# Moving the maxima's transfers from SyncE to ScalarE, and a new order of the last stores and evictions

## The chip, the cores and the metric

The kernel runs on one core of one Trainium2 chip. The metric is the device time of one execution, in microseconds. Before the change the median of three runs is 1801.67 us (1796.04 to 1801.83).

Five engines run their own instruction streams and meet through semaphores: TensorE (PE in the profile), VectorE (DVE), ScalarE (ACT), GpSimd (POOL) and SyncE (SP, which here only issues transfers).

## The reference, cut to what matters

The input x has 2048 rows of 640. Two things are computed from it and mixed by a gate of one number per row:

```
g = sigmoid((x * gate_w).sum(-1))
a = Cr @ (x @ Wr.T) - Ci @ (x @ Wi.T)          # real part of a 2-D Fourier transform; Cr, Ci 2048 x 2048
q = x @ wq  (32 heads of 20);  k = x @ wk;  v = x @ wv   (one key and value head for all)
p = softmax(q k^T / sqrt(20));  b = (p v) @ wo
out = g * a + (1 - g) * b
```

All of it is float32. The kernel reaches that with a high and a low part of each operand and three products.

## The kernel before, in words

**Attention.** The 32 heads are worked in 16 pairs, and each pair in two halves of the rows, so that there are 32 stages, numbered v = 2p + qh. For each stage two passes over the scores are made. Pass "a" (`a_unit`, L227, matmul L235) computes scores and VectorE reduces each 128 x 512 block to its row maximum (L242). When a stage's 64 blocks are done, `a_reduce` and `a_final` (L244 to L267) join them, transpose, and split the negated maximum into a high and a low part (tile m3). The maxima are then needed as two more rows of the query tile: m3 is stored to a scratch tensor `m_d` in DRAM (L258), and four small reads bring it back, as rows 60, 61, 124 and 125 of `qs[v]` (L261 to L267). Pass "b" (`b_unit`, L854, matmul L857) computes the scores with those rows, so the maximum is already subtracted, and ScalarE takes the exponential (L865). `av_step` multiplies the result with the values (L869). So no matmul of pass b of stage v can start before the four reads have landed.

**The loop.** A stage is eight rounds (L976). A round follows a written list (`AB15`, `Y16`, `Y12`, `N12`, L924 to L942): eight pass-b blocks and eight pass-a blocks (none in `N12`), some 12 to 16 pairs of half-width matmuls of the other work ("y0", "y1"), two evictions on ScalarE (E0, E1) and two av steps (V). Pass a runs ahead: the maxima of stage v + 1 are done at the end of the sixth round of stage v, so two rounds lie between them and their first use. Four times a round `tick` (L216) moves a counter on and calls what `later(n, f, ...)` (L213) has put off by n ticks; it is called behind the 1st, 3rd, 5th and 7th pass-b block.

**The other work** is the Fourier part, a generator (`f_stream`, L778) from which matmuls are drawn: first the product along the hidden dimension (`ab_stream`), then seven products with the 2048 x 2048 matrices, whose blocks `load_c` fetches (512 KB each) and `split_c` splits on GpSimd, and last the output projection of the first 512 columns (L823 on).

**The order.** Line 49 puts TensorE, ScalarE, VectorE and GpSimd under a manual schedule: their instructions run in the order in which the code issues them. SyncE isn't in that list; a planner of the framework orders its transfers. Every transfer of the kernel before goes through SyncE (`move`, L109).

**The end.** The last pair of heads has its sums late. `finish_half` stores them, `finish_last` takes the reciprocals on VectorE and stores them, `load_rec` reads them back spread over partitions, `split_last` multiplies them in and splits the product, and `o_group` does the last 128 columns of the projection: three matmuls, one eviction into the accumulator (L664), one store of the output (L665). The first 16 groups (rows 0 to 1023) run right behind the loop, the other 16 when the second half's reciprocals are there. `split_last` for the first half is called inside the loop, behind the last but one round (kk = 6 of the last stage, L1011 to L1013).

Of the kernel before, what the change touches and what calls it, by code (L numbers as in the profile page):

```python
# [17 lines left out]
P = 128  # L18
# [15 lines left out]
def kernel(  # L34
# [71 lines left out]
    def words(ap):  # L106
        return ap.bitcast(F32) if ap.dtype == F32R else ap

    def move(dst, src):  # L109
        nc.sync.dma_start(words(dst), words(src))  # L110

    def split(raw, hi, lo):
        nc.scalar.activation(hi, raw, AF.Copy)
# [102 lines left out]
    def tick():  # L216
        clock["n"] += 1
        due = [t for t in todo if t[0] <= clock["n"]]
        todo[:] = [t for t in todo if t[0] > clock["n"]]
        for _, f, args in due:  # L220
            f(*args)
# [27 lines left out]
    def a_final(v):  # L249

        m3 = sml[0].tile([P, 3, 32], F32, name="m3")
        nc.vector.transpose(m3[:, 0], mxr[v % 2])
        mt = m3[:, 0].rearrange("p (t o) -> p t o", o=1)
        both = m3[:, :2].rearrange("p i t -> p t i")
        with nc.allow_low_precision(reason="high and low part of the maximum"):
            nc.vector.tensor_reduce(m3[:, 1].bitcast(F32R), mt, axis=AX.X, op=ALU.max, negate=True)
            nc.vector.tensor_reduce(m3[:, 2].bitcast(F32R), both, axis=AX.X, op=ALU.add, negate=True)
        move(m_d[v], m3[:, 1:])  # L258

        m_v = m_d[v].rearrange("(g r) i t -> r i g t", g=4)  # L260
        for hh in range(2):  # L261
            for i in range(2):
                r = 64 * hh + 60 + i
                move(
                    qs[v][r : r + 1].rearrange("o (b g t) -> o b g t", g=4, t=32),
                    m_v[hh * QB : (hh + 1) * QB, i : i + 1].rearrange("b o g t -> o b g t"),
                )  # L267


    sml = []  # L270
    chores = []
# [373 lines left out]
    def split_last(qh, k, n):  # L645
        cs = slice(k * QT // n, (k + 1) * QT // n)
        if k == 0:
            last_hl[qh] = [c_slot(2 * qh + z, [P, QT], F32R, "osp") for z in range(2)]
        o, r = last_o[qh]
        h, l = last_hl[qh]  # L650
        nc.vector.tensor_tensor(o[:, cs], o[:, cs], r[:, cs], op=ALU.mult)
        nc.vector.tensor_copy(h[:, cs], o[:, cs])
        nc.vector.tensor_tensor(l[:, cs], o[:, cs], h[:, cs].bitcast(F32), op=ALU.subtract)

    orot = Rot(["S0", "S1", "S2", "S3", "S4", "F0", "F1"])

    def o_group(tb, e):
        qh, k = divmod(tb, SJ)
        tk = slice(k * P, (k + 1) * P)
        ps = orot(f"o_{tb}_{e}")[:, :HALF]  # L660
        h, l = last_hl[qh]
        mm3(ps, h[:, tk], l[:, tk], *wos[OC, e], 1, 0)
        t = acc[tb][:, e]
        nc.vector.scalar_tensor_tensor(t, ps, omg[:, tb : tb + 1], t, op0=ALU.mult, op1=ALU.add)  # L664
        move(out[tb * P : (tb + 1) * P, e * HALF : (e + 1) * HALF], t)  # L665


    class Halves:
# [66 lines left out]
    def ab_stream():  # L735

        groups = []
        for e in range(2):
            for m in range(SJ):
                k = NT * e + 2 * m  # L740
                turn = [(z, i) for z in range(2) for i in range(2)]
                if m == (SJ - 1, 0)[e]:
                    turn.sort(key=lambda x: x[1])
                groups += [(e, k + z, i) for z, i in turn]
        ends = {}
        for n, (e, k, i) in enumerate(groups):
            ends["x", k] = n
            ends["w", e, i] = n
        wait = [(ends["x", k - 3], 1, 1, load_x, split_x, (k,)) for k in range(3, len(XSEQ))]
        for i in range(2):  # L750
            wait.append((ends["w", 0, i], 0, 2, load_w, split_w, (i, 1)))
        wait.sort(key=lambda x: x[:2])
        flying = [(0, 1, 1, load_x, split_x, (2,))]
        for n, (e, k, i) in enumerate(groups):
            ps = [bank("F", f"ab_{n}_{g}") if stage["loop"] else lrot(f"ab_{n}_{g}") for g in range(2)]
            ps = [x[:, :HALF] for x in ps]
            xh, xl = x_now[k]
            for c in range(KC):
                wh, wl = w_of(i, c)
                halves.put(ps, xh[:, c], wh, c == 0, False)  # L760
                yield ("put", 1)
                halves.put(ps, xl[:, c], wh, False, False)
                yield ("put", 1)
                halves.put(ps, xh[:, c], wl, False, c == KC - 1)
                if c == KC - 1:
                    ended.append({"ab": (e, XSEQ[k], i), "ps": ps})
                yield ("put", 1)
            for _, _, _, _, f2, args in flying:
                f2(*args[: 1 if f2 is split_w else 2])
            flying = []  # L770
            while wait and wait[0][0] <= n and sum(x[2] for x in flying) + wait[0][2] <= 2:
                flying.append(wait.pop(0))
                flying[-1][3](*flying[-1][5])
            if n == len(groups) - 3:
                load_c(0)
                split_c(0)

    def f_stream():  # L778

        yield from ab_stream()  # L780
        cw.close()
        yp.append(ctx.enter_context(tc.tile_pool(name="yp", bufs=2, side="right")))
        for g in range(NP):
            n, k = divmod(g, NT)
            r, sh = divmod(k, 2)
            name = PRODUCTS[n][0]
            if g == 0:
                load_c(1)
            if g >= 2:
                free_c.append(c_now.pop(g - 2)[2])  # L790
            sum_t(g - 1)
            split_c(g + 1)
            load_c(g + 2)
            split_b(g + NT)
            load_b(g + NT + 1)
            if n == 0 or g == NT:
                load_t(g)
            if n == len(PRODUCTS) - 1:
                if 1 <= k <= KC + 1:
                    split_wo(k - 2) if k > 1 else None  # L800
                    load_wo(k - 1)
                elif k in (12, 14):
                    load_o((k - 12) // 2)
                elif k == 13:
                    split_o(0)
            if sh == 0:
                ps = [bank("F", f"y_{name}_{r}_{z}")[:, :HALF] for z in range(2)]
                parts = [part(z, part_d[x][r]) for z, x in enumerate(READS.get(name, ()))]
            h, l, _ = c_now[g]
            for j in range(SJ):  # L810
                t = ab[n % 2, sh * SJ + j]
                hi, lo = t[:, 0], t[:, 1]
                s0 = sh == 0 and j == 0
                s1 = sh == 1 and j == SJ - 1
                halves.put(ps, h[:, j], hi, s0, False)
                yield ("put", 1)
                halves.put(ps, h[:, j], lo, False, False)
                yield ("put", 1)
                halves.put(ps, l[:, j], hi, False, s1)
                if s1:  # L820
                    ended.append({"y": (name, r, parts), "ps": ps})
                yield ("put", 1)
        for tb in range(NT):  # L823
            for e in range(2):
                if e == 0:
                    split_o(tb + 1)
                else:
                    load_o(tb + 2)
                ps = [bank("F", f"oo_{tb}_{e}_{z}")[:, :HALF] for z in range(2)]
                y0 = part(e, y_d[tb * P : (tb + 1) * P, e * HALF : (e + 1) * HALF])  # L830
                h, l = osp[tb]
                for c in range(OC):
                    wh, wl = wos[c, e]
                    halves.put(ps, h[:, c], wh, c == 0, False)
                    yield ("put", 1)
                    halves.put(ps, h[:, c], wl, False, False)
                    yield ("put", 1)
                    halves.put(ps, l[:, c], wh, False, c == OC - 1)
                    if c == OC - 1:
                        ended.append({"o": (tb, e, y0), "ps": ps})  # L840
                    yield ("put", 1)
# [175 lines left out]

    for i in range(NT):
        tb, e = divmod(i, 2)
        o_group(tb, e)  # L1020
        if i == 1:
            for st in old:
                av_step(*st)
            finish_half(*old[-1][:2])
            load_last(1)
        elif i >= NT - 4:
            tick()
    load_rec(1)
    for i in range(NT):
        tb, e = divmod(i, 2)  # L1030
        if i % 4 == 0:
            split_last(1, i // 4, 4)
        o_group(SJ + tb, e)


# [45 lines left out]
```

## Time and profile before

| | |
|---|---|
| median of the runs | 1801.67 us |
| profiled execution, its time / its span | 1803.36 us / 1801.6 us |
| TensorE matmul busy | 1747.6 us (97%) |
| VectorE busy | 1372.5 us (76%) |
| ScalarE busy | 1243.0 us (69%) |
| GpSimd busy | 1123.1 us (62%) |
| mean granted TensorE clock | 0.985 |
| transfers, all issued by SyncE | 260.52 MB, 145 GB/s |

The busy shares are means over stages that differ. Where an engine's idle time comes from is read from the waits and from the timeline; what a stage loses is read by laying stages with the same number of matmuls side by side. In a row of a timeline the two first numbers are the start and the duration in us, and the bracket at the end says how long the engine was idle before, and what ended it.

### The profile page before, as it was taken

Reading aid. Unit: us, or ns where it says so; the run is one execution under the profiler, and the core shown is the slowest. Engines: PE = TensorE matmul, PEld = TensorE weight load, DVE = VectorE, ACT = ScalarE, POOL = GpSimd, SP = SyncE. Lnnn points to the kernel's source line nnn. Section 1 sums busy time; section 2 is a strip of 40 time slices with the busy share of each in tenths; the row PEclk is TensorE's granted clock in tenths of the full one; section 3 lists DMA queues with packets and bytes.
Section 4 is the critical chain, followed back from the end, with each engine's and each line's share of the span. In section 5 each row is a group of like instructions: output and inputs, shape, how many; then the busy total and the mean of one; then the engine's idle time right before and its main releaser. Section 6 shows DMA issues by size and latency. Waiting matters only on the chain.

```text
span 1801.6 us, 43713 instructions
## 1 busy us (share of the span) xinstructions
PE 1747.6 (97%) x16728; PEld 1246.0 (69%) x16728; DVE 1372.5 (76%) x2301; ACT 1243.0 (69%) x2470; POOL 1123.1 (62%) x983
## 2 busy tenths in 40 slices
PE   8999999999999999999999989999999999999995
PEld 6797767767677677677767667776776666666664
DVE  4498888888788688788868768886888788888814
ACT  3337887887677677577767657666777777788891
POOL 3056563332878656777868897897887443367781
PEclk9999999999999999999999999999999999999998
DMA  7552232222776433456657764654455222132334
GB/s 245 184 168 77 75 98 81 75 77 90 232 232 207 155 108 106 155 191 208 221 175 234 229 218 145 197 182 152 156 175 167 79 82 77 39 89 78 87 102 137
DMA packets 175059, 260.52 MB, mean 145 GB/s; under 512 B 32330, under 2 KB 131146, under 8 KB 174250
## 3 DMA queue, kind: packets, MB, share of 16 engines
q1 hardware_dynamic: 174850, 257.74, 45.7%
q8 instruction: 131, 2.15, 0.5%
q14 instruction: 78, 0.64, 0.1%
HBM read 184.59 MB, written 77.00 MB: 145 GB/s over the span
## 4 chain that ended last, share of the span: by engine, by line
PE 92%; DMA 4%; SPq 1%; POOL 1%; DVE 1%; issue 0%; ACT 0%; DVEq 0%; POOLq 0%; ACTq 0%
PE av L869 25%; PE b L857 18%; PE y_p L680 18%; PE a L235 15%; PE ab L680 7%; PE oo L680 3%; DMA m_d<-m 2%; PE q L118 1%; PE q L120 1%; SPq L110 1%; PE q L119 1%; DMA qs<-m_d 1%; DMA wraw<-in_wq_dram 1%; POOL cl L504 1%; DVE acc L664 0%
## 5 line engine op out<-in xcount | busy, mean ns | idle before, releaser
L242 DVE TENSOR_REDUCE mx<-a 128x1 f32<-128x512 f32 x2048 | 1278.4, 684 | 309.5 <-PE a L235 285.3
L865 ACT ACTIVATE pt<-b 128x512 f32<-128x512 f32 x2048 | 1076.7, 605 | 395.0 <-PE a L235 326.6
L857 PE MATMUL b<-qs,ks 62*128 62x512 f32 x2048 | 782.0, 419 | 23.5 <-DMA qs<-m_d 20.5
L235 PE MATMUL a<-ks,qs 60*128 60x512 f32 x2048 | 728.5, 414 | 0.0
L680 PE MATMUL y_p<-tb,ch 64*128 64x320 f32 x3584 | 642.9, 310 | 0.0
L857 PEld LDWEIGHTS b<-qs,ks 62*128 62x128 f32 x2048 | 355.2, 187 | 251.4 <-DVE mx L242 163.9
L680 PEld LDWEIGHTS y_p<-tb,ch 64*128 64x128 f32 x3584 | 488.6, 188 | 8.6 <-POOL ch L503 0.3
L869 PE MATMUL av<-pt,vsb 128*32 128x512 f32 x4096 | 492.5, 598 | 0.0
L680 PE MATMUL y_p<-tb,cl 64*128 64x320 f32 x1792 | 450.7, 309 | 1.9 <-POOL cl L504 1.9
L235 PEld LDWEIGHTS a<-ks,qs 60*128 60x128 f32 x2048 | 354.2, 186 | 8.3 <-issue 1.1
L722 POOL TENSOR_TENSOR yt<-yt,yu 128x320 f32<-128x320 f32 x88 | 76.6, 870 | 345.1 <-ACT yu L717 325.9
L680 PEld LDWEIGHTS y_p<-tb,cl 64*128 64x128 f32 x1792 | 280.0, 188 | 7.7 <-POOL cl L504 2.1
L504 POOL TENSOR_TENSOR cl<-craw,ch 128x1024 fp32r<-128x1024 f32 x112 | 267.5, 2388 | 9.0
L869 PEld LDWEIGHTS av<-pt,vsb 128*32 128x32 f32 x4096 | 106.8, 109 | 223.7 <-issue 214.9
L722 POOL TENSOR_TENSOR abt<-abt,abu 128x320 f32<-128x320 f32 x64 | 55.8, 871 | 181.0 <-ACT abu L717 170.4
L498 POOL TENSOR_TENSOR craw<-craw 128x1024 f32<-128x1024 f32 x64 | 153.5, 2398 | 0.0
L503 POOL CAST ch<-craw 128x1024 fp32r<-128x1024 f32 x112 | 116.2, 1038 | 12.8 <-PE a L235 6.5
L680 PE MATMUL oo<-wo,osp 64*128 64x320 f32 x768 | 93.2, 307 | 0.0
L680 PEld LDWEIGHTS oo<-wo,osp 64*128 64x128 f32 x768 | 85.8, 186 | 1.8
L522 POOL TENSOR_TENSOR tb<-braw,tb 128x320 fp32r<-128x320 f32 x80 | 70.1, 876 | 6.4
L680 PE MATMUL ab<-wbh,xh 64*128 64x320 f32 x256 | 58.8, 306 | 0.0
L680 PE MATMUL ab<-wbh,xl 64*128 64x320 f32 x256 | 58.5, 305 | 0.0
(111 smaller groups left out, 1622.2 us busy)
## 6 DMA issues: line engine op xcount, KB each, us to landing
craw<-in_cre_dram SPq DMA_DIRECT2D x80, 512.0 KB
craw<-in_cim_dram SPq DMA_DIRECT2D x64, 512.0 KB
s_d<-craw SPq DMA_DIRECT2D x32, 512.0 KB
craw<-s_d SPq DMA_DIRECT2D x32, 512.0 KB
braw<-b_d SPq DMA_DIRECT2D x80, 160.0 KB
xraw<-in_xT_dram SPq DMA_DIRECT2D x32, 320.0 KB
qs<-qh_d SPq DMA_DIRECT2D x128, 80.0 KB
b_d<-abt SPq DMA_DIRECT2D x64, 160.0 KB
```

Source lines behind the costliest of these rows:

```text
L110: nc.sync.dma_start(words(dst), words(src))
L235: nc.tensor.matmul(ps, qs[v][b : b + 60, qb * P : (qb + 1) * P], ks[b : b + 60, c * ROW : (c + 1) * ROW], start=True, stop=True,)
L242: nc.vector.tensor_reduce(mx[v][:, hh, qb, c : c + 1], ps, axis=AX.X, op=ALU.max)
L498: nc.gpsimd.tensor_tensor(raw[0], raw[0], raw[1], op=how)
L503: nc.gpsimd.tensor_copy(h, raw[0])
L504: nc.gpsimd.tensor_tensor(l, raw[0], h.bitcast(F32), op=ALU.subtract)
L522: nc.gpsimd.tensor_tensor(t[:, 1], raw, t[:, 0].bitcast(F32), op=ALU.subtract)
L680: nc.tensor.matmul(ps, w, x, start=start, stop=stop)
L722: nc.gpsimd.tensor_tensor(t0, t0, t1, op=ALU.add)
L857: nc.tensor.matmul(ps, ks[b : b + 62, kc * P : (kc + 1) * P], qs[2 * p + qc // 2][b : b + 62, (qc % 2) * ROW : (qc % 2 + 1) * ROW], start= ...
L865: nc.scalar.activation(t, ps, AF.Exp, scale=SCALE)
L869: nc.tensor.matmul(ps[32 * g : 32 * g + 32, :], vsb[:, kc, :], t, start=first, stop=last)
```

## The change

`a_final` no longer issues its five transfers at once on SyncE. The store to `m_d` is put off by one tick, the reads by 4, 5, 5 and 6 ticks, and ScalarE issues them. `load_c` of the Fourier part is called two ticks later, except that of block 1, which moves into `ab_stream`. In `split_last` the rounding copy goes to ScalarE, and the multiplication goes to GpSimd for all but the first piece. The first 16 output stores are issued by ScalarE, two groups late; the ticks that issue the reciprocals move behind the loop of groups; every third of the last 16 groups is evicted by ScalarE (scaled copy) and GpSimd (addition) instead of VectorE.

```
+    def move_act(dst, src):
+        nc.scalar.dma_start(words(dst), words(src))
...
-        move(m_d[v], m3[:, 1:])
+        later(1, move_act, m_d[v], m3[:, 1:])
...
-                move(
+                later(
+                    4 + hh + i,
+                    move_act,
                     qs[v][r : r + 1].rearrange("o (b g t) -> o b g t", g=4, t=32),
...
-        nc.vector.tensor_tensor(o[:, cs], o[:, cs], r[:, cs], op=ALU.mult)
-        nc.vector.tensor_copy(h[:, cs], o[:, cs])
+        (nc.gpsimd if k else nc.vector).tensor_tensor(o[:, cs], o[:, cs], r[:, cs], op=ALU.mult)
+        nc.scalar.activation(h[:, cs], o[:, cs], AF.Copy)
...
+    def o_store(i, how):
+        tb, e = divmod(i, 2)
+        how(out[tb * P : (tb + 1) * P, e * HALF : (e + 1) * HALF], acc[tb][:, e])
+
-    def o_group(tb, e):
+    def o_group(tb, e, spread):
...
-        nc.vector.scalar_tensor_tensor(t, ps, omg[:, tb : tb + 1], t, op0=ALU.mult, op1=ALU.add)
-        move(out[tb * P : (tb + 1) * P, e * HALF : (e + 1) * HALF], t)
+        if spread:
+            u = yp[0].tile([P, HALF], F32, name="yt")
+            nc.scalar.activation(u, ps, AF.Copy, scale=omg[:, tb : tb + 1])
+            nc.gpsimd.tensor_tensor(t, t, u, op=ALU.add)
+        else:
+            nc.vector.scalar_tensor_tensor(t, ps, omg[:, tb : tb + 1], t, op0=ALU.mult, op1=ALU.add)
...
             if n == len(groups) - 3:
                 load_c(0)
                 split_c(0)
+            elif n == len(groups) - 2:
+                load_c(1)
...
-            if g == 0:
-                load_c(1)
...
-            load_c(g + 2)
+            later(2, load_c, g + 2)
...
     for i in range(NT):
         tb, e = divmod(i, 2)
-        o_group(tb, e)
+        o_group(tb, e, False)
...
-        elif i >= NT - 4:
-            tick()
+        elif i > 1:
+            o_store(i - 2, move_act)
+    for _ in range(4):
+        tick()
     load_rec(1)
+    for i in range(NT - 2, NT):
+        o_store(i, move_act)
     for i in range(NT):
-        tb, e = divmod(i, 2)
         if i % 4 == 0:
             split_last(1, i // 4, 4)
-        o_group(SJ + tb, e)
+        o_group(SJ + i // 2, i % 2, i % 3 == 2)
+        o_store(NT + i, move)
```

## The prediction, made before the result was known

> **What bounds the kernel now.** First the page: the whole span, then the engines, the clock and the chain.
>
> ```profile
> span 1801.6 us, 43713 instructions
> PE 1747.6 (97%) x16728; PEld 1246.0 (69%) x16728; DVE 1372.5 (76%) x2301; ACT 1243.0 (69%) x2470; POOL 1123.1 (62%) x983
> PEclk9999999999999999999999999999999999999998
> PE 92%; DMA 4%; SPq 1%; POOL 1%; DVE 1%; issue 0%; ACT 0%; DVEq 0%; POOLq 0%; ACTq 0%
> ```
>
> TensorE is the bound, and the chain of work runs through it for 92%. So nothing is to be had from a faster helper, only from places where TensorE waits or runs slowly. The groups of instructions (busy time, mean ns of one | idle time before them and what ended most of it) and the matmul timeline say where that is in the loop:
>
> ```profile
> L857 PE MATMUL b<-qs,ks 62*128 62x512 f32 x2048 | 782.0, 419 | 23.5 <-DMA qs<-m_d 20.5
> 599.08 0.76 PE L857 MATMUL b<-qs,ks 62*128 62x512 f32 x1 [3.21 <-DMA qs<-m_d]
> 1073.86 0.76 PE L857 MATMUL b<-qs,ks 62*128 62x512 f32 x1 [4.47 <-DMA qs<-m_d]
> ```
>
> Pass b of some stages waits for the maxima's reads, 20.5 us in all. A stall costs more than its wait: the matmul behind it takes 0.76 us where the mean is 419 ns. So I measure stages whole. These windows run from one start of `a_final`'s transpose to the next; the columns are length, then busy time and count of each engine, then granted clock, DMA share, GB/s.
>
> ```profile
> 430.12:482.57 52.45, 50.57 (x512) 35.60 (x508) 41.28 (x70) 36.74 (x74) 31.11 (x27) 1.00 0.62 195
> 532.74:582.92 50.18, 50.18 (x516) 35.77 (x512) 41.23 (x69) 35.65 (x71) 37.62 (x34) 1.00 0.66 206
> 582.92:639.92 57.00, 53.53 (x516) 38.48 (x512) 41.11 (x69) 36.21 (x71) 33.13 (x31) 0.94 0.47 148
> 740.28:796.45 56.17, 53.40 (x516) 38.62 (x512) 41.36 (x69) 36.28 (x71) 38.13 (x30) 0.94 0.60 194
> 896.86:954.40 57.54, 53.45 (x516) 38.29 (x512) 41.11 (x69) 36.19 (x71) 40.44 (x33) 0.94 0.59 186
> 1004.58:1056.44 51.86, 50.72 (x516) 35.87 (x512) 41.00 (x69) 35.85 (x71) 44.06 (x36) 1.00 0.72 235
> 1056.44:1114.50 58.06, 53.38 (x516) 38.34 (x512) 41.37 (x69) 36.16 (x71) 44.11 (x35) 0.94 0.52 167
> 1214.87:1271.85 56.98, 53.10 (x516) 38.06 (x512) 41.10 (x68) 35.95 (x71) 43.26 (x34) 0.94 0.52 161
> 1421.03:1470.50 49.47, 48.96 (x456) 32.38 (x448) 39.94 (x68) 36.49 (x69) 26.55 (x27) 1.00 0.34 104
> 1470.50:1519.23 48.73, 48.73 (x456) 32.52 (x448) 40.15 (x69) 36.10 (x69) 16.96 (x12) 1.00 0.28 85
> ```
>
> With the same 516 matmuls a stage takes 50.18 us undisturbed and 51.86 to 58.06 us in the six disturbed ones. The long ones have a granted clock of 0.94: half of the loss is the wait, the other half is TensorE being slow behind it.
>
> Why are the maxima late? VectorE, then SyncE's queue, in the stage that ends in the stall at 599:
>
> ```profile
> 583.38 0.22 DVE L257 TENSOR_REDUCE m<-m 128x32 fp32r<-128x64 f32 x1
> 591.48 0.33 SPq L110 DMA_DIRECT2D craw<-in_cim_dram  x1
> 592.38 0.38 SPq L110 DMA_DIRECT2D m_d<-m  x1
> 596.25 2.78 SPq L110 DMA_DIRECT2D qs<-m_d  x4
> ```
>
> The maxima are ready at 583.60 and their store is issued at 592.38, 8.8 us later, behind transfers like the block load at 591.48. The reads follow at 596.25, and TensorE goes on at 599.08, about 1.5 us behind the second read (four take 2.78, so two end near 597.6). Two rounds (12.5 us, a quarter of 50.18) lie between maxima and use, and SyncE's queue eats most of them. The transfers themselves are quick.
>
> **The change part by part, as a sum against the profiled execution** (span 1801.6, time 1803.36, which is 1.69 above the median 1801.67).
>
> *Maxima on ScalarE.* The store comes one tick on, the last read six ticks on: one and a half rounds, so 9.4 of 12.5 us, and 1.5 us to land leaves 1.6 us or more. All stalls on `qs<-m_d` should go. Six stages: 57.00 + 56.17 + 57.54 + 51.86 + 58.06 + 56.98 - 6 x 50.18 = 36.5 us. The small one at 1421: 49.47 - 48.73 = 0.7 us. There is no more to gain: the other stages are already fully busy on TensorE (50.18 of 50.18).
>
> *Block 1 loaded earlier.* In the stage from 430.12 TensorE is idle for 52.45 - 50.57 = 1.9 us, and that has one place:
>
> ```profile
> 453.44 0.42 PE L680 MATMUL y_p<-tb,cl 64*128 64x320 f32 x2 [1.88 <-POOL cl L504]
> ```
>
> The load moves ahead by two groups of `ab_stream`, a round or more, so I count all 1.9 us. Loads of later blocks move back by two ticks (3.1 us), which I cost at nothing: GpSimd's splits never waited for a block behind this one, its own waits being for evictions. If that cover is gone, each late block stalls TensorE as here.
>
> *What ScalarE pays.* Five issues per stage, 31 stages. Durations on SyncE, median in the middle:
>
> ```profile
> L110 SPq DMA_DIRECT2D qs<-m_d x128: 641/642/743, 140.7 to 1719.8; - x128
> L110 SPq DMA_DIRECT2D m_d<-m x32: 319/384/1936, 136.9 to 1712.9; - x32
> L865 ACT ACTIVATE pt<-b 128x512 f32<-128x512 f32 x2048 | 1076.7, 605 | 395.0 <-PE a L235 326.6
> 897.77 4.26 ACT L865 ACTIVATE pt<-b 128x512 f32<-128x512 f32 x8 [2.02 <-PE a L235]
> 891.51 4.25 ACT L865 ACTIVATE pt<-b 128x512 f32<-128x512 f32 x8 [1.35 <-PE a L235]
> ```
>
> The seventh round holds store and first read, 0.38 + 0.64 = 1.0 us; the eighth three reads, 1.9 us. Queued behind them are the exponentials, whose end frees pass b's banks, and the evictions E0 and E1. ScalarE is idle for 2.02 or 1.35 us ahead of each round. No row shows an issue on ScalarE, so I bound it. Nothing, if an issue runs while earlier activations run or wait: eight exponentials of 605 ns mean take 4.26 us, so one is taken in before the last ends. Or the full duration: 1.9 us exceed an idle of 1.35 by 0.6 per stage, and in the last stage, where ScalarE is never idle (rows from 1757 below), all 3 us count; I round that up to 0.8 per stage, 25 us in all. I take 4 us, near the lower end, since the idle rows cover nearly the whole price. The Trainium skill's Perfetto Trace Analysis (section on DVE and Act instructions) says that the sequencer pushes an activation into a wait queue and is free for the next; by that rule this term is 0. No row here shows the rule for a transfer.
>
> *The seam before the last round.* `split_last` for the first half puts a multiplication on GpSimd and a copy that needs it on ScalarE, ahead of the last round's exponentials:
>
> ```profile
> 1757.53 4.03 ACT L865 ACTIVATE pt<-b 128x512 f32<-128x512 f32 x8
> 1759.73 0.87 POOL L628 TENSOR_TENSOR acc<-yt,part 128x320 f32<-128x320 f32 x1
> L617 POOL TENSOR_TENSOR oraw<-oraw x16: 1281/1289/1300, 1540.1 to 1746.3; 128x512 f32<-128x512 f32 x16
> ```
>
> In GpSimd's order the multiplication stands behind the accumulation that ends at 1760.6; it ends at 1761.9. The copy holds ScalarE until then, and itself takes 0.5: the exponentials of 1757.53 begin at 1762.4. ScalarE sets the pace there, so the loop ends 4.9 us later.
>
> *Reciprocals first.* Now:
>
> ```profile
> 1770.87 6.49 SPq L110 DMA_DIRECT2D out_dram<-acc  x12
> 1777.45 1.11 SPq L110 DMA_DIRECT2D rec_d<-rc  x2
> 1772.06 0.24 DVE L915 RECIPROCAL rc<-sm 128x16 f32<-128x16 f32 x1
> 1783.03 0.43 DVE L651 TENSOR_TENSOR oraw<-oraw 128x256 f32<-128x256 f32 x1 [10.73 <-DMA oraw<-rec_d]
> ```
>
> The reciprocals end at 1772.30 and their store waits for twelve output stores until 1777.45. With those on ScalarE it saves 5.1 us, no more, since the store and the reading back stay.
>
> *Shared evictions.* The last 16 groups are four quarters:
>
> ```profile
> 1787.73 0.41 DVE L651 TENSOR_TENSOR oraw<-oraw 128x256 f32<-128x256 f32 x1
> 1786.72 1.09 DVE L664 SCALAR_TENSOR_TENSOR acc<-o,omg,acc 128x320 f32<-128x320 f32 x2 [0.25 <-PE o L120]
> 1788.52 0.42 PE L118 MATMUL o<-wo,osp 128*128 128x320 f32 x1 [1.37 <-DVE osp L652]
> 1789.51 1.93 DVE L664 SCALAR_TENSOR_TENSOR acc<-o,omg,acc 128x320 f32<-128x320 f32 x4 [0.58 <-PE o L120]
> 1791.35 0.41 DVE L651 TENSOR_TENSOR oraw<-oraw 128x256 f32<-128x256 f32 x1
> 1757.02 0.61 ACT L717 ACTIVATE yu<-oo,omg 128x320 f32<-128x320 f32 x1
> ```
>
> A quarter takes 1791.35 - 1787.73 = 3.62 us on VectorE. Afterwards the next quarter's multiplication stands on GpSimd behind the shared group's addition: scaled copy 0.61, addition 0.87, multiplication 0.73 (between 128x320 at 0.87 and 128x512 at 1.29, extended down), rounding copy some 0.45, handovers 0.24: 2.9 us behind the shared group's matmuls, which are the third, second and fourth of quarters 1 to 3. In the first quarter the third group's matmuls end at 1786.7, 3.7 us behind the first multiplication (1783.03), and 0.1 later for the slower copy: 3.8 + 2.9 = 6.7 to the next quarter's matmuls, which now start at 5.5 (1788.52). In the others the first group ends 1.0 us behind the quarter's first matmul (1789.51 - 1788.52) and each further one about 0.45 later, so the second ends at 1.4 and the fourth at 2.3: 4.3 and 5.2 against 3.62. So the quarters lengthen by 1.2, 0.7 and 1.6 us. In the last, the third group's addition ends at 1.9 + 0.61 + 0.87 + 0.1 = 3.5, against 2.9 (1789.51 + 1.93 - 1788.52): +0.5. In all +4.0 us.
>
> Tail: +4.9 - 5.1 + 4.0 = +3.8 us. Its bounds: -5.1, if hold and spread cost nothing, to +7, if TensorE also slows in the gaps.
>
> Sum: -36.5 - 0.7 - 1.9 + 4 + 3.8 = -31.3; 1803.36 - 31.3 = 1772; less 1.69, **1770 us** for the median.
>
> **Rivals.**
>
> (1) *Stalls remain in part.* ScalarE's own reads wait for the store to land, and block loads fill the DMA (share 0.72 in the worst stage). Against it: a landing took under 4 us (592.38 to 596.25), and three ticks, 4.7 us, lie between store and first read. If half of the 36.5 remain: 1770 + 18 = 1788.
>
> (2) *ScalarE pays in full*, 25 instead of 4: 1791.
>
> (3) *Slower.* The issues share the machinery that makes descriptors: if each of ScalarE's five has to wait for a SyncE issue in progress and takes the longest one seen, 1.94 us, the eighth round holds 5.8 us against 2.0 idle and the seventh 3.9: 5.7 us per stage beyond the idle, 19 stages with heavy traffic, +108 us: about 1870. It decides from 1.9 us per such stage (35.3 of gain without the 4). Against it: the reads took at most 743 ns among 128, also in heavy traffic. The Perfetto Trace Analysis page of the Trainium skill (HWDGE section) says that an issue locks a shared generator and that the recorded time includes the wait; it makes this rival possible, and no row here has a second issuer to show it.
>
> (4) *The stall only moves.* Blocks come 3.1 us later and TensorE waits for splits instead, as at 453.44. Six stalls of 6 us in 31 stages would use up the gain: 1801, no change. GpSimd is idle for a quarter of each such stage (37.62 of 50.18 busy), which speaks against it.
>
> **How the numbers follow.** Forecast 0.68, (1) 0.12, (2) 0.08, (3) 0.06, (4) 0.06. About 0.3% (5 us) can be told from no change here. Faster holds the forecast, (1) and (2): 0.88; same most of (4): 0.05; slower (3) and the rest: 0.07. The range goes from no cost on ScalarE and the best tail (1801.67 - 39.1 - 5.1 = 1757) to (2): 1758 to 1791.
>
> **What would show it.** No wait of TensorE on `qs<-m_d` above 0.5 us, all stages of 516 matmuls at 50.2 to 50.5 us, clock 1.00: first term right. ScalarE's idle time ahead of the eighth round shrinking, TensorE unmoved: the 4 us right. A gap of some 4 us on ScalarE ahead of its last eight exponentials, waiting for GpSimd: the seam right. The reciprocals' store within 0.5 us of the reciprocals; quarters of 4 to 5 us. The prediction is wrong if rounds with issues stretch, or if a new wait on block splits appears.

## The result, and the profile after

The median rises from 1801.51 us to **1873.81 us** (1870.0 to 1876.25, four runs each): ratio 1.0407, 95% interval 1.038 to 1.0434. The change makes the kernel slower by 4%; 1770 us was forecast.

First the page of the changed kernel (time 1870.0 us, span below): span, engines, granted clock, the chain of waits, and the group of pass b, whose last columns are the idle time before it and what ended most of it.

```profile
span 1868.2 us, 43669 instructions
PE 1767.6 (95%) x16728; PEld 1251.0 (67%) x16728; DVE 1370.1 (73%) x2286; ACT 1254.8 (67%) x2481; POOL 1129.3 (60%) x992
PEclk9999999999999999999999999999999999999997
PE 85%; DMA 5%; POOL 3%; ACT 3%; issue 2%; ACTq 1%; DVE 1%; SPq 1%; POOLq 0%
L868 PE MATMUL b<-qs,ks 62*128 62x512 f32 x2048 | 787.0, 421 | 57.7 <-ACT pt L876 55.8
```

TensorE does the same 16728 matmuls, but the chain leaves it for 15% of the span instead of 8%. Pass b waits longer than before, 57.7 us against 23.5, and no longer for the maxima: it waits for ScalarE's exponentials (`pt`), which free its banks.

Where do the 66.6 us between the two spans lie? I cut both traces at the starts of `a_final`'s transpose, as the prediction did. The 17 stages with heavy block traffic, the prediction's stages with 516 matmuls among them, can be asked as one window. Columns: window, length, busy time and count of PE, PEld, DVE, ACT, POOL, then granted clock, DMA share, GB/s. First before, then after with three single stages.

```profile
482.57:1372.22 889.65, 869.62 (x8708) 621.23 (x8704) 699.38 (x1164) 604.93 (x1195) 684.69 (x547) 0.98 0.57 182
```

```profile
483.26:1422.98 939.72, 880.89 (x8708) 623.24 (x8704) 702.62 (x1165) 609.05 (x1195) 683.94 (x547) 0.97 0.54 172
332.34:382.41 50.07, 49.60 (x500) 35.04 (x496) 41.01 (x70) 39.85 (x82) 15.86 (x16) 1.00 0.25 75
600.19:659.63 59.44, 53.16 (x516) 37.79 (x512) 41.29 (x69) 36.38 (x71) 33.12 (x31) 0.94 0.41 127
659.63:710.90 51.27, 50.61 (x516) 35.80 (x512) 41.35 (x69) 35.33 (x69) 32.74 (x30) 1.00 0.36 107
```

| part of the span | after minus before, us |
|---|---|
| up to the first of these transposes (134.3 and 132.8) | -1.5 |
| seven stages ahead of the heavy ones (348.3 to 350.4) | +2.1 |
| 17 heavy stages | +50.1 |
| seven quiet stages behind them | +5.7 |
| from there to the last evictions ahead of the last round | +1.0 |
| the last round and the tail (43.97 to 53.07) | +9.1 |
| sum | +66.5 |

Two kinds of loss can be told apart. Every stage that ran undisturbed before has become longer: the four lightest heavy stages take 51.13 to 51.41 us against 50.18, a stage at the start 50.07 against some 49.25. And 13 of the 17 heavy stages now take between 52.8 and 60.3 us, where 6 had 51.9 to 58.1 before.

The waits of the changed kernel (total us, times, longest) show who is late in these. The first five end ScalarE's idle time ahead of an exponential with the landing of a transfer:

```profile
ACT pt L876 <- DMA qs<-m_d: 22.2, 6, 7.0
ACT pt L876 <- DMA braw<-b_d: 14.4, 3, 5.8
ACT pt L876 <- DMA craw<-in_cre_dram: 8.5, 2, 5.4
ACT pt L876 <- DMA craw<-s_d: 4.2, 1, 4.2
ACT pt L876 <- DMA part_dp<-yt: 4.0, 1, 4.0
PE b L868 <- ACT pt L876: 55.8, 27, 6.3
```

That is 53.3 us in 13 waits. An exponential reads a bank of scores; it needs none of these tiles. `braw` and `craw` are blocks of the Fourier part. So what waits is not the exponential but the transfer ahead of it in ScalarE's order. (The view names the transfer that raised one of the semaphores last. In the six gaps of the first row ScalarE issued two reads, and the name is that of the earlier one.) The timeline of one such place, all engines:

```profile
600.66 0.22 DVE L260 TENSOR_REDUCE m<-m 128x32 fp32r<-128x64 f32 x1
601.10 0.60 ACT L876 ACTIVATE pt<-b 128x512 f32<-128x512 f32 x1 [2.02 <-PE a L238]
602.56 1.27 SPq L110 DMA_DIRECT2D braw<-b_d  x3
607.11 0.32 ACTq L113 DMA_DIRECT2D m_d<-m  x1
607.54 1.08 ACT L876 ACTIVATE pt<-b 128x512 f32<-128x512 f32 x2 [5.83 <-DMA braw<-b_d]
608.19 0.79 PE L868 MATMUL b<-qs,ks 62*128 62x512 f32 x1 [5.62 <-ACT pt L876]
```

The maxima are ready at 600.88, the store's only data. It goes out at 607.11, when one of the three `braw` loads has landed that SyncE issued from 602.56 on. Until then ScalarE stands still (5.83 us), and with it TensorE (5.62 us), whose next matmul takes 0.79 us where the mean is 421 ns.

The compiled program's listing says why. It gives each transfer of SyncE and ScalarE one of eight completion semaphores (DMAHW0 to DMAHW7) in turn, and lets a transfer wait until the earlier user of its semaphore, eight places before, has landed. For this stage:

```
SyncE    braw <- b_d11   raises DMAHW2 to 1088
SyncE    six more transfers, on DMAHW3 to DMAHW7 and DMAHW0
SyncE    part <- part_dp raises DMAHW1 to 1104
ScalarE  m_d <- m3       raises DMAHW2 to 1104; waits for DVE (its data) and for DMAHW2 at 1088
```

167 of ScalarE's 176 transfers wait in this way, 155 of them for a transfer of SyncE. Before the change all transfers were on SyncE, where such a wait holds up only other transfers.

The trace keeps the time at which each semaphore rises, so the listing can be laid beside it. The `braw` load above has landed at 607.04, and the store goes out 0.07 us later. Of the 13 waits, 12 are of this kind: an issue in the gap starts 0.02 to 0.08 us after the SyncE transfer eight places ahead of it has landed. The thirteenth (1.5 us, at 1271.34) is two issues one behind the other. A read's wait for its own store is rarer: in the heavy stages it held ScalarE four times, with idle times of 2.9 us at most and 5.1 us together.

### The profile page after: what moved, and what is told of

It reads as the page before. It is cut to its first block, busy times and chain, and to the rows that moved or that the text cites. A ratio compares the mean times of both kernels' runs of the same rounds, so it can differ in the third digit from the quotient of the medians.

```text
span 1868.2 us, 43669 instructions
## 1 busy us (share of the span) xinstructions
PE 1767.6 (95%) x16728; PEld 1251.0 (67%) x16728; DVE 1370.1 (73%) x2286; ACT 1254.8 (67%) x2481; POOL 1129.3 (60%) x992
## 4 chain that ended last, share of the span: by engine, by line
PE 85%; DMA 5%; POOL 3%; ACT 3%; issue 2%; ACTq 1%; DVE 1%; SPq 1%; POOLq 0%
PE av L880 23%; PE b L868 17%; PE y_p L691 17%; PE a L238 14%; PE ab L691 7%; ACT pt L876 2%; PE oo L691 2%; PE q L121 1%; PE q L123 1%; PE q L122 1%; ACTq L113 1%; POOL craw L501 1%; POOL cl L507 1%; DMA wraw<-in_wq_dram 1%; DMA t_d<-braw 1%
## 5 line engine op out<-in xcount | busy, mean ns | idle before, releaser
L868 PE MATMUL b<-qs,ks 62*128 62x512 f32 x2048 | 787.0, 421 | 57.7 <-ACT pt L876 55.8
L691 PE MATMUL y_p<-tb,ch 64*128 64x320 f32 x3584 | 650.2, 311 | 0.0
```

The lines of the kernel that those rows point to most:

```text
L691: nc.tensor.matmul(ps, w, x, start=start, stop=stop)
L868: nc.tensor.matmul(ps, ks[b : b + 62, kc * P : (kc + 1) * P], qs[2 * p + qc // 2][b : b + 62, (qc % 2) * ROW : (qc % 2 + 1) * ROW], start= ...
```

## The experiments

**Theory A**, formed from these rows: the trips are held on ScalarE by the completion semaphores that they share with SyncE's transfers; the exponentials behind them are held too. The rivals were that the issues themselves cost the time (their duration, or the machinery that both issuers share), that the transfers wait for their own data (the reads for the store), and that other parts of the change (the tail, the block loads) carry the loss. The expectations name rivals by letters where they use them.

To compare the kernels I use the same 17 stages in each: their length, less 17 x 50.18 = 853.1 us, is what they lose against an undisturbed stage. Before it was 36.6 us, after it is 86.7 us.

**1. The trips back on SyncE, the rest as changed.**

```
-        later(1, move_act, m_d[v], m3[:, 1:])
+        move(m_d[v], m3[:, 1:])
...
-                later(
-                    4 + hh + i,
-                    move_act,
+                move(
```

> The changed kernel with the maxima's store and reads put back as they were: issued at once, by SyncE. All else of the change stays. If ScalarE's issues are the loss (every one of the theories below), ScalarE's waits for transfers vanish and what is left is the tail and the seam in the Fourier part: the stretch from the last transpose of a_final to the end was 89.4 us before and 99.5 us in the changed kernel, some 3 us of that being issues on ScalarE, so 1801.5 + 7 - 2 = about 1806 us, with stalls of TensorE on the reads as before. Rival: the later block loads or the shared evictions carry the loss; then it stays near 1870 us.

1815.32 us (1812.66 to 1817.72), ratio to the kernel before 1.0074 [1.0051, 1.0097]. The trips on ScalarE cost 58 us of the 72. Windows, then the tile `m_d` (who waited for it):

```profile
478.27:1374.18 895.91, 869.82 (x8708) 620.59 (x8704) 699.88 (x1165) 605.57 (x1195) 685.07 (x547) 0.98 0.57 181
```

```profile
L110 SPq DMA_DIRECT2D qs<-m_d x128: 641/642/1158, 139.1 to 1722.9; - x128
  PE b L866: 27.2, 15
```

The stalls on the maxima are back: 895.91 - 853.1 = 42.8 us lost, somewhat more than before (36.6). The rest of the change alone makes the kernel slower by 0.7%, 9 us more than I expected; the tail is taken up below.

**2. The trips alone, the rest as before.** The kernel before, with the five transfers of `a_final` put off and issued by ScalarE as in the change.

> The kernel before with one part of the change alone: store and reads issued by ScalarE, 1 and 4, 5, 5, 6 ticks on. If ScalarE's issues are the loss: about 1867 us (1873.8 less some 7 us of the tail). Rival (other parts): about 1762 us, the forecast without the tail.

1856.70 us (1853.59 to 1859.79), 1.0304 [1.0279, 1.033]: +57.0. With the +15.6 of run 1 that is 72.6, the whole of the loss, so the two parts hardly interact. The time is 10 us below the 1867 us that I had written down, and 95 us above the rival's 1762.

```profile
486.91:1418.34 931.43, 878.74 (x8708) 623.16 (x8704) 702.45 (x1165) 609.88 (x1195) 684.64 (x547) 0.97 0.54 173
```

78.4 us are lost in the 17 stages.

**3. Transfers that nobody reads.** The kernel before, maxima on SyncE as ever; at the same ticks ScalarE issues five transfers of the same shapes from inputs to a scratch tensor. Nothing of the computation is left out, and nothing depends on them.

```
+        later(1, move_act, idle_d[v, 0], ident[:, :64])
+        x_v = xT[:P, :64].rearrange("(g r) (i t) -> r i g t", g=4, i=2)
+        for hh in range(2):
+            for i in range(2):
+                later(
+                    4 + hh + i,
+                    move_act,
+                    idle_d[v, 1 + 2 * hh + i, :16].rearrange("(o p) t -> o (p t)", o=1).rearrange(
+                        "o (b g t) -> o b g t", g=4, t=32
+                    ),
+                    x_v[hh * QB : (hh + 1) * QB, i : i + 1].rearrange("b o g t -> o b g t"),
+                )
```

> The kernel before, maxima on SyncE as they were, and beside them five transfers per stage on ScalarE at the ticks of the change, of the same shapes, that copy inputs to a scratch tensor nobody reads. They wait for no result and nothing waits for them: what they cost is the issue and any wait that is not for data. Theory A (an issue on ScalarE waits until an earlier transfer of SyncE, which was given the same one of eight completion semaphores, has landed): ScalarE waits for SyncE's transfers in the stages with heavy traffic, up to 6 us at a time, and the time is 1850 us or more. Theory B (the loss is ScalarE's first read waiting for its own store to land): no waits here, only issues, 31 stages x 1 us: 1815 to 1832 us, with all stages alike. Theory C (issues alone, a generator shared with SyncE): no waits for transfers, but issues longer than 0.65 us in heavy stages.

1871.49 us (1865.76 to 1879.89), 1.0390 [1.0347, 1.0433]: as slow as the change. Windows, the tile of the idle transfers (min, median, max ns), a wait, and the timeline of ScalarE at the place shown above:

```profile
486.72:1423.97 937.25, 886.46 (x8708) 620.47 (x8704) 703.03 (x1164) 608.72 (x1195) 684.89 (x547) 0.98 0.54 173
```

```profile
L114 ACTq DMA_DIRECT2D idle_d<-in_xT_dram x128: 661/662/1287, 133.5 to 1786.2; - x128
L114 ACTq DMA_DIRECT2D idle_d<-ident x32: 321/321/361, 130.8 to 1779.8; - x32
```

```profile
ACT pt L882 <- DMA idle_d<-in_xT_dram: 24.9, 10, 4.6
```

```profile
602.55 0.32 ACTq L114 DMA_DIRECT2D idle_d<-ident  x1
602.98 1.09 ACT L882 ACTIVATE pt<-b 128x512 f32<-128x512 f32 x2 [5.41 <-DMA braw<-b_d]
```

A store of constants waits for a `braw` load, 5.41 us with the exponential behind it. It has no data to wait for, and its only wait in the listing is the shared semaphore: of these 160 transfers 154 wait so, 126 of them for a transfer of SyncE. The ten waits that carry the idle transfers' own name are named as above: in seven of the gaps the first issue starts 0.02 to 0.03 us after a SyncE transfer has landed, and the other three, 0.9 us each, are two issues one behind the other. So the trips' own data aren't the cause, and the 17 stages lose 84 us all the same. Nor is the duration of an issue: it is 0.32 and 0.66 us in the median and never over 1.29. Theory A stands.

**4. The trips on GpSimd**, whose transfers have completion semaphores of their own (DMASW0 to DMASW7 in the listing), the rest as changed: `move_pool`, a transfer issued by GpSimd, for `move_act` in `a_final`.

> The changed kernel with the maxima's store and reads issued by GpSimd at the same ticks; its transfers have completion semaphores of their own, which SyncE's do not use. Theory A: no wait for SyncE's transfers; ScalarE runs as before; stalls of TensorE on the reads mostly gone; about 1775 us if GpSimd's idle quarter covers five issues per stage. Theory B: GpSimd's first read waits for the store instead, splits and evictions behind it come late, and TensorE waits for them: above 1800 us.

1926.89 us (1925.29 to 1931.39), 1.0698 [1.0672, 1.0723]: a miss by 150 us. The tile `m_d` of this kernel: durations, then its engine's waits, then who waited for it.

```profile
L116 POOL DMA_DIRECT2D qs<-m_d x128: 538/553/601, 139.7 to 1832.1; - x128
  DVE m L263: 30.1, 8
  DMA m_d<-m: 29.9, 13
  PE b L871: 105.3, 31
```

No transfer of SyncE is among what GpSimd waits for here, in keeping with A. But the reads come too late, and TensorE waits for them 105.3 us. GpSimd works in order, and the issues stand behind its splits (2.4 us each) and behind additions that wait for evictions:

```profile
993.98 2.41 POOL L510 TENSOR_TENSOR cl<-craw,ch 128x1024 fp32r<-128x1024 f32 x1
...
999.11 0.87 POOL L736 TENSOR_TENSOR yt<-yt,yu 128x320 f32<-128x320 f32 x1 [1.36 <-ACT yu L731]
...
1001.84 0.58 POOL L116 DMA_DIRECT2D m_d<-m  x1
```

GpSimd also stands still itself, 30.1 us for the maxima and 29.9 us for the store, ahead of the first read; this last wait, and a time above 1800 us, are what theory B of the expectation named. I had counted the price of the issue and not the order it joins: the same omission as in the prediction, on another engine. ScalarE with semaphores of its own wasn't tried, since the framework hands them out.

**5 and 6. Earlier maxima instead of another issuer.** The kernel before, with pass a one round (6.3 us) or two further ahead:

```
-    LEAD = 10
+    LEAD = 14        # 18 in the other run
```

> The kernel before with one number changed: pass a runs 14 units ahead of the loop instead of 10, so that each stage's maxima are ready one round (about 6.2 us) earlier; SyncE issues everything, as before. If the stalls of the kernel before come from the maxima's trip being late on SyncE, and cost 37 us as the stages say: the waits of TensorE on the reads (at most 4.5 us) go, and with some 2 us more work ahead of the loop the time is about 1766 us. Rival: SyncE's queue is late by as much again, or the stalls move to the splits; then it stays within 10 us of 1800.

> The same with 18 units, two rounds earlier. If one round is enough, no gain over 14 units, and about 2 us more for the work ahead of the loop: 1768 us. If SyncE is late by more than a round, better than 14 units by what is left of the stalls.

1767.17 us (1765.12 to 1768.6), 0.9811 [0.9788, 0.9834], and 1770.38 us (1767.65 to 1771.3), 0.9827 [0.9804, 0.985]. Both as expected. With 14:

```profile
479.04:1332.97 853.93, 853.93 (x8708) 608.42 (x8704) 699.17 (x1165) 603.27 (x1197) 681.72 (x544) 1.00 0.59 190
```

The 17 stages lose 0.9 us instead of 36.6, TensorE is busy for every one of the 853.93 us, and the clock is at 1.00. So the gain that the prediction priced at 36.5 us was there to be had, on SyncE, by giving the trip more time. A second round more brings nothing.

**7. The tail's arithmetic back on VectorE.** Run 1, with `split_last`'s multiplication and copy and all last evictions on VectorE as before; the reciprocals first and the stores on ScalarE stay.

```
-        (nc.gpsimd if k else nc.vector).tensor_tensor(o[:, cs], o[:, cs], r[:, cs], op=ALU.mult)
-        nc.scalar.activation(h[:, cs], o[:, cs], AF.Copy)
+        nc.vector.tensor_tensor(o[:, cs], o[:, cs], r[:, cs], op=ALU.mult)
+        nc.vector.tensor_copy(h[:, cs], o[:, cs])
...
-        o_group(SJ + i // 2, i % 2, i % 3 == 2)
+        o_group(SJ + i // 2, i % 2, False)
```

> The changed kernel with maxima on SyncE as before, and also the multiplication, the rounding copy and all evictions of the last groups back on VectorE; output stores on ScalarE, reciprocals' order and block loads stay as in the change. Compared with the run that only put the maxima back (1815 us): if the seam before the last round (5.3 us in the trace) and the longer quarters (5.0 us) are the shared work's doing, 1805 us. Rival: the late sums make the tail long; then about 1813 us.

1807.69 us (1803.62 to 1809.62, ten runs), 1.0031 [1.0018, 1.0045]. Against run 1 (by the ratios, 0.43%) the tail's sharing costs 7.7 us; the time is nearer the 1805 us of the expectation than its rival's 1813. What is left, with the seam of block 1 gained and the reciprocals earlier, is still 0.3% above the kernel before. Its trace shows where it differs from the trace before: the 17 stages lose 3.8 us more (893.41 against 889.65), the seven stages ahead of them are 2.4 us shorter (345.85 against 348.30), and from the last transpose to the end it takes 89.92 us against 89.40. So the reciprocals' order gains nothing there. The profiled run (1803.70 us) is 4 us faster than this kernel's median, so most of the 0.3% stays open.

**8. What is left of the change, with the earlier maxima.** The kernel before with LEAD 14, `load_c(1)` moved into `ab_stream`, and the first 16 output stores issued by ScalarE behind `load_rec`, so that the reciprocals are stored first; no trips on ScalarE, no shared evictions.

> A version meant to beat both: pass a 14 units ahead, SyncE issues the maxima, block 1 loaded two groups early, other blocks as before; in the tail all arithmetic as before, and the first 16 output stores issued by ScalarE only behind the reading back of the reciprocals. Expected: the gain of 14 units (to 1766 us), less 2.5 us at the Fourier seam, less 4 to 5 us for the reciprocals' store no longer behind twelve stores: about 1759 us. If the tail's gain is eaten by transfers in competition, 1763 us.

**1763.58 us** (1762.96 to 1766.12), 0.9794 [0.9772, 0.9817]: the fastest of all, 3.6 us below LEAD 14 alone in the median; the intervals of the two overlap. Of the two values written down it is the second, 1763, and not 1759: the tail's gain did not come. From the last transpose to the end it takes 94.86 us, with LEAD 14 alone 94.56. What is gained lies in the seven stages ahead of the heavy ones, where block 1 is needed (343.39 us against 347.83).

## Why the prediction was wrong

**The stalls on the maxima, -37.2: right in itself.** No wait of TensorE on `qs<-m_d` is left in the changed kernel, and the run with LEAD 14 shows what it is worth when nothing else is added (34.8 us). It isn't visible in the result only because something larger came in.

**What ScalarE pays, +4 with an upper bound of 25: this step failed.** It has two parts.

The issues. Quiet stages grow by 0.7 to 1.2 us; with the 1.06 of the heavy ones (below) it is about 0.95 in 31 stages, some 30 us. My lower end rested on issues that "run while earlier activations run or wait". These rows of a quiet stage after the change say otherwise:

```profile
718.10 0.60 ACT L876 ACTIVATE pt<-b 128x512 f32<-128x512 f32 x1 [1.15 <-PE a L238]
718.12 1.35 ACTq L113 DMA_DIRECT2D qs<-m_d  x2
719.57 1.09 ACT L876 ACTIVATE pt<-b 128x512 f32<-128x512 f32 x2 [0.87 <-PE y_p L691]
```

The issues begin when the activation before them has begun, 0.02 us on, and the next activation begins 0.10 us after their end (718.12 + 1.35 = 719.47). They don't use the idle time ahead of an activation (1.15 us before the first); they make idle time of their own, and part of it reaches TensorE. (The view puts the 0.87 us down to TensorE; that the issues make it is read from the times. With the trips back on SyncE, run 1, the seven quiet stages behind the heavy ones take 340.7 us instead of 345.7.) By itself this part came out near my upper bound: 30 against 25.

The waits. They are in no term and no bound of mine. By estimate, of the 86.7 us that the 17 stages lose, 17 x 1.06 = 18 go to the issues (1.06 is the mean of the four lightest stages, 51.24, less 50.18), and 69 to the waits shown above: 53.3 us of standing still on ScalarE (the held issues' own time is in it) and the slow matmuls behind them. Together ScalarE's price is 30 + 69 = 99 us instead of 4. (The spans give the same: 66.6 us longer, less the 9.1 of the tail, plus the 37.2, the 2.5 of block 1 and the 1.5 ahead of the first transpose, is 98.7.) The unstated premise was that a transfer leaves SyncE's queue when another engine issues it. It left the queue and kept the semaphores.

Here I had also picked the wrong rule. The prediction weighed what the Trainium skill's Perfetto Trace Analysis says of activations (section DVE / Act Engine Instruction: they are pushed into a wait queue and the sequencer is free). A transfer on ScalarE follows the same page's section DMA Instruction — HWDGE: the sequencer itself sits through the semaphore wait, and the recorded time starts only when it is over. The rows agree with that one: the issue at 607.11 is recorded with 0.32 us, and the 5.83 us ahead of it show up as idle time of the exponential.

**Rival (3), slower, about 1870,** names the right sum for the wrong reason; that the number fits is luck. It let each issue lock the shared machinery for 1.94 us. The tile of the trips, after (min, median, max ns of the reads):

```profile
L113 ACTq DMA_DIRECT2D qs<-m_d x128: 653/654/1247, 135.0 to 1777.2; - x128
```

They take 0.65 us in the median, against 0.64 on SyncE, and none took 1.94. Its threshold was sound: 1.9 us in each of 19 heavy stages would use up the gain, and 87 / 17 = 5.1 us were lost. Rival (1) falls, since no stall on the maxima remains (its wait for the store shows up on ScalarE instead, the 5.1 us above); rival (2) is the first half of what happened; rival (4) falls, since TensorE waits for no split.

**Block 1 earlier, -1.9: right.** The stage took 52.45 us before; it takes 50.78 after, 49.94 in run 1, without the issues: 2.5 us.

**The tail, +3.8: it is +9.1.** The timeline of the changed kernel, all engines:

```profile
1814.52 0.61 ACT L728 ACTIVATE yu<-oo,omg 128x320 f32<-128x320 f32 x1
1818.48 1.26 POOL L654 TENSOR_TENSOR oraw<-oraw 128x512 f32<-128x512 f32 x1
1819.77 0.63 ACT L655 ACTIVATE osp<-oraw 128x512 fp32r<-128x512 f32 x1 [4.13 <-POOL oraw L654]
1820.31 4.00 ACT L876 ACTIVATE pt<-b 128x512 f32<-128x512 f32 x8
1828.69 0.60 ACT L891 ACTIVATE ob<-av 128x512 f32<-128x512 f32 x1 [3.56 <-PE av L880]
1828.76 8.52 ACTq L113 DMA_DIRECT2D out_dram<-acc  x16
1829.32 1.53 SPq L110 DMA_DIRECT2D sum_d<-ob  x4
1836.02 1.12 SPq L110 DMA_DIRECT2D sm<-sum_d  x2
1838.92 0.25 DVE L926 RECIPROCAL rc<-sm 128x16 f32<-128x16 f32 x1 [3.13 <-DMA sm<-sum_d]
1839.20 1.10 SPq L110 DMA_DIRECT2D rec_d<-rc  x2
1844.57 0.43 DVE L654 TENSOR_TENSOR oraw<-oraw 128x256 f32<-128x256 f32 x1 [5.39 <-DMA oraw<-rec_d]
```

- *The seam, +4.9: right.* The last exponentials start 5.2 us behind the evictions (1820.31 against 1815.13), before it was -0.1: +5.3, with GpSimd's multiplication as the cause, as foretold. 1.1 us more go to slow matmuls behind the hold, which I had only in the bound.
- *Reciprocals first, -5.1: half of it.* Their store follows them within 0.3 us, as foretold (1838.92, 1839.20). But from the last `ob` to the first multiplication of `split_last` it is 15.9 us (1828.69 to 1844.57) against 18.2 before (1764.83 to 1783.03): -2.3. The sums are read back 6.7 us after their store was issued; before it was 2.65 (1765.46 to 1768.11):

```profile
1765.46 1.12 SPq L110 DMA_DIRECT2D sum_d<-ob  x4
1768.11 1.11 SPq L110 DMA_DIRECT2D sm<-sum_d  x2
```

  ScalarE's 16 output stores go out in the same 8.5 us. It is again a shared semaphore, with SyncE waiting this time. The last of the sums had landed at 1832.28; the reading back is issued at 1836.02, 0.02 us after the output store eight places ahead of it has landed. The list of SyncE's waits has it as the longest of three:

```profile
SPq L110 <- DMA out_dram<-acc: 3.4, 3, 2.5
```

  In runs 7 and 8, which also store from ScalarE, the sums are read back 7.0 and 7.6 us after their store; with LEAD 14 alone it is 2.66. It fits that neither run gained anything in the tail. How much later the output stores themselves land because of the traffic isn't separated.
- *Shared evictions, +4.0:* from the first multiplication to the end 23.6 us (1844.57 to 1868.2) against 18.6 (1783.03 to 1801.6): +5.0. The way was right, the size a quarter too small. From quarter to quarter it is +0.9, +0.4, +2.7 and +1.1, where +1.2, +0.7, +1.6 and +0.5 were forecast. In the third quarter two groups are shared, the first and the fourth (i = 8 and 11), and the prediction's sum has only the fourth; its matmuls also take 0.47 us where they took 0.31.

Run 7 confirms the two losses together: undoing seam and sharing gives 7.7 us back, of the 11.4 (5.3 + 1.1 + 5.0) that the trace puts down to them.

Of the sum, then: the range 1758 to 1791 missed, since its upper end was rival (2), and 0.07 for slower was far too little. "Rounds with issues stretch" was named as what would prove the prediction wrong; it did.

## What to carry to other kernels

Before you move a transfer to an engine that computes, look in the listing for what the transfer will wait for, its completion semaphore included: on SyncE a wait holds up other transfers, on a computing engine everything behind it in order stands still. The Trainium skill (DMA: Bandwidth & Descriptors, section Issuing engines are not separate DMA queues) says that issuing on several engines saves only the sequencer's time; here even that was paid for on ScalarE. And where data is late for its use, first make it earlier: one constant gave 35 us that the moved transfers could not.

## What the runs showed of the hardware that was not expected

- An issue on ScalarE that no landing holds mostly starts right behind the start of the activation ahead of it (0.02 us behind it at 718.10; within 0.08 us in 80 of 121 such issues), and mostly the next activation starts after the issue's end (in 119 of all 160; not everywhere: behind the issue of 994.07, 0.66 us long, one starts at 994.51). Five issues of 2.9 us together (0.32 + 4 x 0.65) lengthen a stage by some 1 us.
- The same read costs an issuer about the same: 0.64 us on SyncE, 0.65 on ScalarE, 0.55 on GpSimd; the store 0.38, 0.32 and 0.58.
- A stop costs more than it lasts. In the 17 heavy stages after the change TensorE stood idle for 58.8 us (939.72 - 880.89), and its matmuls took 27.8 us more than undisturbed (880.89 - 853.1), about half as much again; the granted clock is 0.94 in the five longest of these stages.
